# Widening the weight-sum matmuls of the shared key slot from 32 to 64 columns in a masked-attention and two-layer kernel

## The chip, the cores and the metric

The kernel runs on one core of one Trainium2 chip. The metric is the device time of one execution in microseconds (us); lower is better. Engines are named as in the profile: PE (TensorE matmul), PEld (its weight loads), DVE (VectorE), ACT (ScalarE), POOL (GpSimd), SP (the engine that issues the transfers).

## The reference

Attention over 4 batches x 8 heads, 576 positions, head size 64. Scores under a threshold below the row's maximum are dropped before the softmax. Its result (2304 tokens x 512) goes through two layers, each up to 2048 and down to 512: softplus in the first, squared ReLU in the second.

```python
scores = scale * np.matmul(q, k.transpose(0, 1, 3, 2))
thresh = np.max(scores, axis=-1, keepdims=True) - tau
scores = np.where(scores >= thresh, scores, -1000000000.0)
scores = scores - np.max(scores, axis=-1, keepdims=True)
attn = np.exp(scores)
attn = attn / (np.sum(attn, axis=-1, keepdims=True) + 1e-09)
return np.matmul(attn, v)
...
g = np.maximum(h, 0.0) + np.log1p(np.exp(-np.abs(h)))   # first layer, h = x @ w_in
...
r = np.maximum(h, 0.0); g = r * r                       # second layer
return g @ w_out
```

## The kernel before, in words

**Units.** The attention is cut into 32 units. A unit is one batch, one half of the query positions (288 of 576) and one pair of heads. Keys lie on the 128 partitions, queries along the free axis. Of a head's 576 keys, 512 fill four slots of 128 partitions. The last 64 keys of both heads share one slot: head 0 has partitions 0 to 63, head 1 has 64 to 127. So a unit's weights after the exponential, tile `st` (called `e` in the code that reads it), have nine slots of 128 x 288: 0 to 3 for head 0, 4 the shared one, 5 to 8 for head 1.

**Output of a unit (`a_out`).** Two PSUM banks take it. Bank `a_ps[0]` (X) sums weights times values: head 0 on partitions 0 to 63, head 1 on 64 to 127. Bank `a_ps[1]` (D) sums the weights alone with a tile of ones, `one_t`: head 0 on partitions 64 to 127, head 1 on 0 to 63. In D each head has two strips of 32 partitions: slots c = 0 and 2 are summed in one, 1 and 3 in the other. The shared slot adds to the first strip only. Later the two strips are read by DVE and ACT (lines 440 to 444), added and inverted.

The matmuls of a unit come in this order on PE, or with the first two groups exchanged, as the planner has it:

- L420: 8 matmuls, 128 rows x 64 columns of the array, into X.
- L427: 8 matmuls, 128 rows x 32 columns, into D, four strips in turn.
- L432 and L433, the shared slot, for head 0 and then head 1: one matmul into X of 64 rows x 64 columns, one into D of 64 rows x 32 columns. All four are one entry of the plan, so that nothing comes between them.

These matmuls are in full float32, and the trace shows each as two MATMUL and two LDWEIGHTS records. The text calls the two the passes of a matmul. The shared slots of all units make 4 matmuls x 2 passes x 32 units = 256 MATMUL records. The rows of the trace write the shape of the array as rows\*columns (64\*32).

**Around it.** An attention unit's weights are made by scores on PE (L364, L369), copied out by ACT (L372), reduced to a maximum by DVE, the maximum goes through DRAM to all partitions, DVE subtracts and thresholds (L402, L405), ACT takes the exponential (L406). The output of unit u is worked out two units after its scores. ACT then copies X and D out (L435, L437); DVE works out the reciprocals (L440 to L446) and scales (L447). Between units' matmuls stand those of the first layer: up (L463 to L465), softplus on ACT and DVE, a split into a high and a low part (ACT L481; DVE or POOL L482), and down (L494 to L496). The second layer has the rest of the time, from about 716 us on.

**What sets the order.** A planner (`Plan`) takes each operation with a cost written into the code and lists them once per engine; the chip runs each engine's list in that order, and semaphores do the rest. The shared slot has the cost 590 ns there.

Of the kernel before, what the change touches and what calls it, by code (L numbers as in the profile page):

```python
# [9 lines left out]
F32 = mybir.dt.float32  # L10
# [6 lines left out]
B, H, S, D = 4, 8, 576, 64  # L17
# [200 lines left out]
def kernel(ctx: ExitStack, tc: tile.TileContext, qT, kT, vp, tau, w1i, w1o, w2i, w2o, out):  # L218
    nc = tc.nc
    w1i, w1o, w2i, w2o = (w.bitcast(U32) for w in (w1i, w1o, w2i, w2o))  # L220
    PE, ACT, DVE, POOL, SP = nc.tensor, nc.scalar, nc.vector, nc.gpsimd, nc.sync
# [37 lines left out]
    ap = att.enter_context(tc.tile_pool(name="att", bufs=1))  # L259
# [14 lines left out]
    NX = 5  # L274
    xf_t = many(NX, [128, HALF], "xf")
    w_t = ap.tile([128, 18], F32, name="w_t")
    one_t = ap.tile([128, 32], F32, name="one_t")
    POOL.memset(one_t, 1.0)
    m_d = [dram.tile([18, 32], F32, name=f"m_d{i}") for i in range(4)]


# [126 lines left out]
    def a_out(u, key):  # L408
        cold = COLD if u < NCOLD else 1
        e, E = st_t[u % 3], [("st", u % 3, o) for o in range(2)]  # L410
        vt, V = v_t[u % 2], ("v", u % 2)
        xf, XF = xf_t[u % NX], ("xf", u % NX)
        rb, RB = rb_t[0], "rb"
        half = [slice(0, 64), slice(64, 128)]
        X, D = a_ps[0][:, :HALF], a_ps[1][:, :HALF]
        AX0, AD = ("a", 0), ("a", 1)
        for c in range(4):
            def mms(c=c):
                for o in range(2):
                    PE.matmul(X[64 * o:64 * o + 64], vt[:, 256 * o + 64 * c:256 * o + 64 * c + 64], e[:, 5 * o + c], start=(c == 0), stop=False)  # L420
            P.add("PE", (490 + 100 * (c == 0)) * cold, mms, E + [V], [AX0], key)
        for c in range(0, 4, 2):
            def mms(c=c):
                for o in range(2):
                    for i in range(2):
                        a = 64 - 64 * o + 32 * i
                        PE.matmul(D[a:a + 32], one_t, e[:, 5 * o + c + i], start=(c == 0), stop=(c == 2 and i == 1))  # L427
            P.add("PE", (490 + 100 * (c == 0)) * cold, mms, E, [AD], key)

        def mms():  # L430
            for o, h in enumerate(half):
                PE.matmul(X[h], vt[h, 512:], e[h, 4], start=False, stop=True)  # L432
                PE.matmul(D[64 - 64 * o:96 - 64 * o], one_t[h], e[h, 4], start=False, stop=True)  # L433
        P.add("PE", 590 * cold, mms, [E[0], V], [AX0, AD], key)
        P.add("ACT", 310, lambda: ACT.copy(xf, X), [AX0], [XF], key - 0.5)  # L435
        for o in range(2):
            P.add("ACT", 310, lambda o=o: ACT.copy(rb[half[o]], D[half[1 - o]]), [AD], [RB], key - 0.5)  # L437

        d, DN = d_t[u % 2], ("d", u % 2)
        P.add("DVE", 380, lambda: DVE.tensor_reduce(d[:, 0], rb.rearrange("p (b i) -> p b i", i=32), axis=AX.X, op=ALU.max, apply_transpose=True), [RB], [DN], key + 1)  # L440
        for a in range(4):
            b = a ^ 1
            P.add("ACT", 220, lambda a=a, b=b: ACT.copy(d[32 * a:32 * a + 32, 1], d[32 * b:32 * b + 32, 0]), [DN], [("d2", u % 2)], key + 0.5)
        P.add("DVE", 140, lambda: DVE.scalar_tensor_tensor(out=d[:, 0], in0=d[:, 0], scalar=1e-9, in1=d[:, 1], op0=ALU.add, op1=ALU.add), [("d2", u % 2)], [DN], key + 1)
        P.add("DVE", 140, lambda: DVE.reciprocal(d[:, 0], d[:, 0]), [], [DN], key + 1)
        P.add("DVE", 380, lambda: DVE.transpose(rb, d[:, 0].unsqueeze(2).to_broadcast([128, 9, 32])), [DN], [RB], key + 1)  # L446
        P.add("DVE", 375, lambda: DVE.tensor_tensor(xf, xf, rb, op=ALU.mult), [RB], [XF], key + 1, lock=True)  # L447
# [67 lines left out]
    with tc.manual_schedule():  # L515
# [5 lines left out]
        for s in range(last1 + 1):  # L521
# [18 lines left out]
            while wpos < len(wlist) and wpos < 2 * (s + 1):  # L540
                src, f, o = wlist[wpos]
# [152 lines left out]
```

## Time and profile before

| | us |
|---|---|
| median of 3 runs | 1174.6 |
| lowest, highest | 1174.29, 1176.4 |
| the profiled execution's own time | 1177.02 |
| its span, first to last instruction | 1175.2 |

Mean granted TensorE clock of the profiled execution: 0.988 of full speed. The span is what the trace covers; 1.8 us of the execution's own time lie around it. Below, "the stretch 230 to 716" is from 230 us to 716 us after the span's start.

### The profile page before, as it was taken

The page shows a single profiled execution, that of the slowest core. Times are in us where ns is not written, and L with a number is a line of the kernel's source. Part 1 is how long each engine was busy: PE and PEld are TensorE (multiplying, and loading weights), DVE is VectorE, ACT ScalarE, POOL GpSimd, SP SyncE. Part 2 cuts the span into 40 slices and gives each one's busy share as a digit, 9 for nine tenths or more (in the row PEclk, how much of TensorE's full clock was granted, in tenths as well). Part 3 has the DMA queues.
Part 4 walks back from the last instruction along what each step waited for, and adds up shares of the span by engine and source line. Part 5 has one row for each costly group of instructions (what it writes and reads, how often), then busy time and mean ns, then how long its engine had stood idle before and what let it go on. Part 6 is the DMA issues. An engine that isn't in the chain of part 4 may idle for free.

```text
span 1175.2 us, 18185 instructions
## 1 busy us (share of the span) xinstructions
PE 1145.8 (98%) x6992; PEld 887.8 (76%) x6992; DVE 698.6 (59%) x992; ACT 690.8 (59%) x1640; POOL 245.6 (21%) x209
## 2 busy tenths in 40 slices
PE   7779999999999999999999999999999999999998
PEld 3335777877877877877777879988888888888887
DVE  5999986766776666657656745889322322222232
ACT  6787887777777776777677657865322222222222
POOL 1024223332332232333223211444000000000000
PEclk9888999999999999999999999999999999999999
DMA  5365422112112112112111004765010010000010
GB/s 190 109 200 181 140 89 84 46 44 81 46 39 83 41 45 83 39 48 74 47 48 42 31 11 146 212 205 159 7 66 1 1 54 1 1 37 1 1 37 19
DMA packets 39291, 81.85 MB, mean 70 GB/s; under 512 B 6180, under 2 KB 14884, under 8 KB 39204
## 3 DMA queue, kind: packets, MB, share of 16 engines
q1 hardware_dynamic: 39204, 80.69, 21.6%
q8 instruction: 55, 0.90, 0.3%
q14 instruction: 32, 0.26, 0.1%
HBM read 71.17 MB, written 9.50 MB: 69 GB/s over the span
## 4 chain that ended last, share of the span: by engine, by line
PE 90%; DVE 4%; ACT 3%; DMA 1%; issue 0%; SPq 0%; ACTq 0%; DVEq 0%
PE h_ps L463 12%; PE h_ps L464 11%; PE h_ps L465 11%; PE y_ps L494 6%; PE y_ps L604 6%; PE y_ps L603 6%; PE y_ps L605 6%; PE y_ps L496 5%; PE y_ps L495 5%; PE a_ps L364 5%; PE a_ps L420 5%; PE a_ps L432 3%; PE a_ps L433 3%; PE a_ps L427 3%; DVE st L402 1%; PE a_ps L369 1%
## 5 line engine op out<-in xcount | busy, mean ns | idle before, releaser
L482 POOL TENSOR_TENSOR g_l<-gt,g_h 128x288 fp32r<-128x288 f32 x96 | 102.8, 1074 | 316.4 <-ACT g_h L481 278.8
L463 PE MATMUL h_ps<-x_h,wih 128*128 128x288 f32 x512 | 160.1, 313 | 0.7 <-DVE gt L476 0.7
L494 PE MATMUL y_ps<-g_h,woh 128*128 128x288 f32 x512 | 158.2, 309 | 0.0
L464 PE MATMUL h_ps<-x_l,wih 128*128 128x288 f32 x512 | 150.5, 294 | 1.2 <-DVE x_l L454 1.2
L465 PE MATMUL h_ps<-x_h,wil 128*128 128x288 f32 x512 | 151.6, 296 | 0.0
L496 PE MATMUL y_ps<-g_l,woh 128*128 128x288 f32 x512 | 151.1, 295 | 0.0
L495 PE MATMUL y_ps<-g_h,wol 128*128 128x288 f32 x512 | 150.9, 295 | 0.0
L402 DVE TENSOR_TENSOR st<-st,mb 64x288 f32<-64x288 f32 (+1 forms) x128 | 129.0, 1022 | 3.3 <-DMA mb<-m_d 2.2
L583 ACT ACTIVATE r<-h_ps 128x512 f32<-128x512 f32 (+1 forms) x80 | 44.5, 556 | 146.2 <-PE h_ps L465 145.8
L584 DVE SCALAR_TENSOR_TENSOR r<-h_ps,r 128x512 f32<-128x512 f32 (+1 forms) x80 | 51.0, 638 | 131.8 <-ACT r L583 131.6
L464 PE MATMUL h_ps<-y_l,wih 128*128 128x512 f32 (+1 forms) x320 | 120.1, 375 | 0.1
L590 ACT CAST g_h<-r 128x512 fp32r<-128x512 f32 (+1 forms) x80 | 46.2, 578 | 125.4 <-PE y_ps L604 125.4
L463 PE MATMUL h_ps<-y_h,wih 128*128 128x512 f32 (+1 forms) x320 | 119.2, 372 | 0.0
L465 PE MATMUL h_ps<-y_h,wil 128*128 128x512 f32 (+1 forms) x320 | 118.7, 371 | 0.0
L591 DVE TENSOR_TENSOR g_l<-r,g_h 128x512 fp32r<-128x512 f32 (+1 forms) x80 | 51.7, 646 | 110.9 <-ACT g_h L590 110.8
L604 PE MATMUL y_ps<-wol,g_h 128*128 128x512 f32 x288 | 114.1, 396 | 0.0
L603 PE MATMUL y_ps<-woh,g_h 128*128 128x512 f32 x288 | 114.1, 396 | 0.0
L605 PE MATMUL y_ps<-woh,g_l 128*128 128x512 f32 x288 | 114.0, 396 | 0.0
L463 PEld LDWEIGHTS h_ps<-x_h,wih 128*128 128x128 f32 x512 | 96.4, 188 | 21.9 <-issue 18.7
L494 PEld LDWEIGHTS y_ps<-g_h,woh 128*128 128x128 f32 x512 | 96.4, 188 | 16.4 <-issue 15.3
L405 DVE SCALAR_TENSOR_TENSOR st<-st,thr 128x1152 f32<-128x1152 f32 (+1 forms) x64 | 104.1, 1628 | 0.1
L476 DVE SCALAR_TENSOR_TENSOR gt<-h_ps,a_t 128x288 f32<-128x288 f32 x128 | 57.4, 450 | 77.3 <-ACT a_t L475 73.9
(102 smaller groups left out, 2410.5 us busy)
## 6 DMA issues: line engine op xcount, KB each, us to landing
k_r<-in_kT SPq DMA_DIRECT2D x32, 320.0 KB
v_t<-in_vp SPq DMA_DIRECT2D x32, 288.0 KB
wraw<-in_w1i SPq DMA_DIRECT2D x16, 512.0 KB
wraw<-in_w1o SPq DMA_DIRECT2D x16, 512.0 KB
wraw<-in_w2i SPq DMA_DIRECT2D x16, 512.0 KB
wraw<-in_w2o SPq DMA_DIRECT2D x16, 512.0 KB
mb<-m_d SPq DMA_DIRECT2D x28, 288.0 KB
q_r<-in_qT SPq DMA_DIRECT2D x32, 144.0 KB
```

Of the source, the lines that this page charges most:

```text
L402: DVE.tensor_tensor(st[p0:p1, a:a + n], st[p0:p1, a:a + n], mb[p0:p1, o:o + 1].to_broadcast([p1 - p0, n, HALF]), op=ALU.subtract),
L405: P.add("DVE", 315 * (s1 - s0), lambda x=x: DVE.scalar_tensor_tensor(out=x, in0=x, scalar=thr, in1=x, op0=ALU.is_lt, op1=ALU.subtract), [] ...
L463: PE.matmul(bank, wih[p][:, c, f], xh[c], start=(c == 0), stop=False)
L464: PE.matmul(bank, wih[p][:, c, f], xl[c], start=False, stop=False)
L465: PE.matmul(bank, wil[p][:, c, f], xh[c], start=False, stop=(c == 3))
L482: P.add(eng, ns, lambda j=j: e.tensor_tensor(g_hl[1][j], gt_t[j], f32(g_hl[0][j]), op=ALU.subtract), [("gt", j), ("g_h", j)], [("g_l", j)] ...
L494: PE.matmul(o, woh[p][:, j, es], g_h[j], start=first, stop=False)
L495: PE.matmul(o, wol[p][:, j, es], g_h[j], start=False, stop=False)
L496: PE.matmul(o, woh[p][:, j, es], g_l[j], start=False, stop=last)
L603: PE.matmul(o, g_h[j][:, ts], woh[p][:, j], start=first, stop=False)
L604: PE.matmul(o, g_h[j][:, ts], wol[p][:, j], start=False, stop=False)
L605: PE.matmul(o, g_l[j][:, ts], woh[p][:, j], start=False, stop=last)
```

## The change

The ones tile gets 64 columns: 32 ones and 32 zeros. It is filled by two POOL instructions instead of one. The matmuls of L427 take its first 32 columns, as before. The two of the shared slot that sum the weights (L433) take all 64 columns and write 64 partitions of D: the first strip of the head gets the sum, and zeros are added to its second strip. The mark that ends an accumulation moves from L427 to L433. No cost and no entry of the plan is changed: on PE, DVE, ACT and SP every instruction keeps its place; the 64 weight-sum matmuls have 64 partitions out in place of 32, and POOL has one instruction more near its start.

```diff
-    one_t = ap.tile([128, 32], F32, name="one_t")
-    POOL.memset(one_t, 1.0)
+    one_t = ap.tile([128, 64], F32, name="one_t")
+    POOL.memset(one_t, 0.0)
+    POOL.memset(one_t[:, :32], 1.0)
...
-                        PE.matmul(D[a:a + 32], one_t, e[:, 5 * o + c + i], start=(c == 0), stop=(c == 2 and i == 1))
+                        PE.matmul(D[a:a + 32], one_t[:, :32], e[:, 5 * o + c + i], start=(c == 0), stop=False)
...
                 PE.matmul(X[h], vt[h, 512:], e[h, 4], start=False, stop=True)
-                PE.matmul(D[64 - 64 * o:96 - 64 * o], one_t[h], e[h, 4], start=False, stop=True)
+                PE.matmul(D[64 - 64 * o:128 - 64 * o], one_t[h], e[h, 4], start=False, stop=True)
```

So the four matmuls of the shared slot have these rows and columns of the array: before, X of head 0 (rows 0-63, columns 0-63), D of head 0 (0-63, 64-95), X of head 1 (64-127, 64-127), D of head 1 (64-127, 0-31); after, the second and the fourth have columns 64-127 and 0-63.

## Rows read from the trace of the kernel before

**Rows 1.** The page: busy us of each engine, share of the span, instructions.

```profile
PE 1145.8 (98%) x6992; PEld 887.8 (76%) x6992; DVE 698.6 (59%) x992; ACT 690.8 (59%) x1640; POOL 245.6 (21%) x209
```

**Rows 2.** Busy time in three stretches: stretch, length, engines' busy us, granted clock, DMA.

```profile
0.00:125.00 125.00, 101.06 (x487) 54.10 (x487) 110.32 (x145) 99.15 (x242) 27.11 (x26) 0.89 0.51 165
125.00:230.00 105.00, 104.25 (x754) 78.51 (x753) 86.36 (x129) 81.81 (x206) 31.87 (x25) 1.00 0.30 91
230.00:330.00 100.00, 100.00 (x739) 78.53 (x738) 65.83 (x94) 74.00 (x193) 31.66 (x26) 1.00 0.17 55
```

**Rows 3.** One shared slot, PE in order of time, pass by pass: start, us.

```profile
580.59 0.45 PE L432 MATMUL a_ps<-st,v_t 64*64 64x288 f32 x1
580.88 0.40 PE L432 MATMUL a_ps<-st,v_t 64*64 64x288 f32 x1
581.22 0.43 PE L433 MATMUL a_ps<-st,one_t 64*32 64x288 f32 x1
581.48 0.40 PE L433 MATMUL a_ps<-st,one_t 64*32 64x288 f32 x1
581.82 0.45 PE L432 MATMUL a_ps<-st,v_t 64*64 64x288 f32 x1
...
583.04 0.40 PE L494 MATMUL y_ps<-g_h,woh 128*128 128x288 f32 x1
```

**Rows 4.** Passes of L427, L420 and L364, in order of time: start, us.

```profile
575.61 0.45 PE L427 MATMUL a_ps<-st,one_t 128*32 128x288 f32 x4
575.88 0.43 PE L427 MATMUL a_ps<-st,one_t 128*32 128x288 f32 x4
...
576.36 0.43 PE L427 MATMUL a_ps<-st,one_t 128*32 128x288 f32 x4
576.72 0.40 PE L369 MATMUL a_ps<-q_h,k_h 128*128 128x288 f32 x1
...
579.03 0.41 PE L420 MATMUL a_ps<-st,v_t 128*64 128x288 f32 x2
579.28 0.41 PE L420 MATMUL a_ps<-st,v_t 128*64 128x288 f32 x2
...
586.82 0.40 PE L364 MATMUL a_ps<-q_h,k_h 64*128 64x288 f32 x2
```

**Rows 5.** All weight loads and passes of L432 and L433: min/median/max ns.

```profile
L432 PEld LDWEIGHTS a_ps<-st,v_t x128: 129/131/133, 36.5 to 704.7; 64*64 64x64 f32 x128
...
L433 PEld LDWEIGHTS a_ps<-st,one_t x128: 102/104/106, 37.1 to 705.3; 64*32 64x32 f32 x128
```

**Rows 6.** The chain that ended last, near the fourth and fifth shared slots: start, us.

```profile
78.36 4.35 DMA wraw<-in_w1o
...
83.50 0.40 ACT rb L437
...
106.26 0.63 PE a_ps L432 x2
```

**Rows 7.** L433 alone in two stretches: stretch, length, PE busy, PEld busy.

```profile
0.00:125.00 125.00, 6.69 (x20) 1.34 (x20) 0.89 0.51 165
125.00:230.00 105.00, 6.69 (x20) 1.34 (x20) 1.00 0.30 91
```

**Rows 8.** Exponentials on ACT and their first readers on PE, ninth and 23rd unit.

```profile
193.76 1.27 ACT L406 ACTIVATE st<-st,qsc 128x1152 f32<-128x1152 f32 x1
...
195.08 0.45 PE L427 MATMUL a_ps<-st,one_t 128*32 128x288 f32 x4
...
502.10 1.50 ACT L406 ACTIVATE st<-st,qsc 128x1440 f32<-128x1440 f32 x1
...
507.86 0.45 PE L427 MATMUL a_ps<-st,one_t 128*32 128x288 f32 x4
```

**Rows 9.** Waits in the stretch 230 to 716: us in total, times, longest.

```profile
ACT rb L437 <- PE a_ps L433: 67.9, 21, 6.5
```

**Rows 10.** Low parts made by POOL: all as a group; one, and its reader.

```profile
L482 POOL TENSOR_TENSOR g_l<-gt,g_h 128x288 fp32r<-128x288 f32 x96 | 102.8, 1074 | 316.4 <-ACT g_h L481 278.8
...
536.36 2.84 POOL L482 TENSOR_TENSOR g_l<-gt,g_h 128x288 fp32r<-128x288 f32 x1 [6.68 <-DVE st L402]
...
539.37 0.29 PE L496 MATMUL y_ps<-g_l,woh 128*128 128x288 f32 x1
```

**Rows 11.** The tile of ones: the fill on POOL.

```profile
L278 POOL MEMSET one_t<- x1: 114/114/114, 1.4 to 1.4; 128x32 f32 x1
```

## The prediction, made before the changed kernel was run

> **What bounds the kernel now.** I read the busy times first. PE is busy 1145.8 us of the span, DVE and ACT some 60% each [rows 1]. An average can hide stages, so the next view is the table of stretches [rows 2]. It shows three parts of the attention phase. From 0 to 125 us PE is busy 101.06 of 125 us and DVE 110.32: here DVE, ACT and transfers lead. From 125 to 230 PE is nearly full, but DVE (86.36 of 105) and ACT (81.81) are not far behind. In the third row, and in those like it up to 716 us, PE is full, DVE has about a third free and ACT a quarter. There a microsecond taken from PE is a microsecond off the end, as long as nobody else is late. The granted clock is 1.00 from 125 us on, the upper level of 2.4 GHz.
>
> Then the one place that the change touches, pass by pass [rows 3]. The shared slot begins at 580.59 and the next work starts at 583.04: 2.45 us for eight passes. The reader should see that no two passes start together. Within one matmul the second pass starts 0.29 us after the first (580.59 to 580.88), and the next matmul, which has another shape, starts 0.34 us after that (580.88 to 581.22). Compare the weight sums of the full slots [rows 4]: four passes on four different column strips start together at 575.61, four more at 575.88, and the fourth such round starts at 576.36, two rounds after the second. So sixteen passes take four rounds, 0.24 us apart, and the next shape begins 0.36 us after the last round (576.72). L420, with two tiles of 64 columns, goes in rounds of two every 0.25 us. L364, with two row tiles, starts two together as well. So passes on different tiles of one shape run side by side here, and where the shape changes they don't.
>
> **The change part by part.** *The shared slot.* Afterwards its four matmuls have one shape, 64\*64, and the four lie on four different quarters of the array. If they behave like the four strips of L427, the first passes start together, the second passes 0.29 us later (the gap in [rows 3]), and the next shape 0.34 us after that. That makes 0.63 us; L427's rounds give 0.27 + 0.36 = 0.63 too. I add 0.02 for a spread of the starts, my choice: 0.65. The slot falls from 2.45 to 0.65 us, 1.80 us a unit. No row has four tiles of 64\*64, so both ends: at best 0.61 (the gaps of the narrower L433, 0.26 from 581.22 to 581.48 and 0.34 from 581.48 to 581.82, give 0.60); at worst all eight passes one after another, priced under the rivals. I take the value near the best because L427, L420 and L364 [rows 4] all run their tiles side by side, and L427 and L364 between them show both ways of cutting, columns and rows.
>
> *Dearer loads.* L433's weight loads take 104 ns at 32 columns, L432's 131 ns at 64 [rows 5]. That is 27 ns for each of 128 loads, 3.5 us if nothing hid them. In L427 and L420 rounds follow each other at 0.24 to 0.25 us with loads in between, so I cost them at nothing; without that cover they are the 3.5 us.
>
> *The second fill.* It stands on POOL beside one that takes 114 ns at 1.4 us [rows 11], some 35 us before the first pass of L433 [rows 5]. Nothing; if it were on the path, 0.1 to 0.2 us.
>
> *Added zeros, later end mark.* No instruction more on PE, and the readers of D waited for L433 already [rows 9]. Nothing.
>
> *What becomes of 1.80 us a unit.* A unit has four passes of L433. Twenty of the 128 fall in the stretch 0 to 125, twenty in 125 to 230 [rows 7], so five units each, and 22 units behind that. I make three groups.
>
> Units 1 to 4: the chain does not run through their slots. At the fourth it lies on a transfer of weights from 78.36 to 82.71 [rows 6], while the slot runs. I count 0; if all counted it were 4 x 1.80 = 7.2.
>
> Units 5 to 10: the fifth slot is the first on the chain, at 106.26 [rows 6], and from there the slots are on PE's full stretch, but the exponential comes hardly earlier than PE wants it. In the ninth unit it ends at 193.76 + 1.27 = 195.03, and its first reader starts at 195.08 [rows 8]. A PE that arrives 1.80 us earlier waits. ACT and DVE do start earlier behind a shorter slot, so not all is lost. Between 0 and 10.8 us I take the middle: 5.4.
>
> Units 11 to 32, 22 of them: 39.6 us. Here the margin is large. The smallest that I found among the 22 is at unit 23: the exponential ends at 502.10 + 1.50 = 503.60 and is read at 507.86, 4.26 us later [rows 8]. Between a unit's scores and its output lie the slots of two other units, so a faster PE can use up at most 3.6 us of it, even if the whole chain through ACT and DVE took no profit. And it does profit: in this stretch ACT's next copy waited 67.9 us, in 21 waits, for the last pass of the slot [rows 9], so ACT moves up along with PE. What can bite is the hand-over inside the first layer. Mostly it has microseconds to spare, but POOL's low part that ends at 536.36 + 2.84 = 539.20 is read at 539.37, 0.17 us later [rows 10]. I take off a tenth, 4.0 us, as an estimate for such places: 35.6.
>
> *Sum:* 0 + 5.4 + 35.6 = 41.0 us. The profiled execution's own time of 1177.02 becomes 1136.0. It stood 2.4 us above the median of the runs, 1174.6, so I forecast **1133.6 us**. Everything counted, 32 x 1.80 = 57.6, would give 1117.0; the second stretch at 0 and a quarter lost in the third, 29.7, gives 1144.9.
>
> **The rivals.**
>
> *Two at a time.* Both matmuls into X write one bank, from different halves of the rows, and so do both into D. L364's two row tiles, which do run together, write two different banks; L427's four strips share a bank but have all the rows. So no row shows two row tiles in one bank at once. If the bank holds the second row tile back, the order X, D of head 0, then X, D of head 1 gives two pairs of rounds: 0.29 + 0.24 + 0.25 + 0.34 = 1.12 us. The saving is 1.33 a unit; weighed as above, 41.0 x 1.33 / 1.80 = 30.3, or 1144.3 us. For it: the gap in the rows just named. Against it: the two write different partitions, as L427's strips do, and those don't hold each other back. The Trainium skill's page TensorEngine Tiling, section Restrictions and Gotchas, bears on this: it says that different row tiles cannot access the same PSUM bank simultaneously, and leaves the order to software. By that rule the slot would be the 1.12 us just given; the trace of before neither shows nor breaks it.
>
> *One after another.* The tiles gain nothing from a common shape, only the waits at the three changes of shape inside the slot shrink: 0.29 + 6 x 0.245 + 0.34 = 2.10 us. That saves 0.35 a unit, 41.0 x 0.35 / 1.80 = 8.0 us, 1166.6. This is the case in which the change doesn't do what it says. Against it stand all the rounds of [rows 4].
>
> *Eaten by DVE and ACT.* The slot shortens, but PE then waits for exponentials or low parts. Shorter by 41 us or so, the 125 to 716 stretch would ask for more of DVE and ACT in each microsecond, and POOL's work beside DVE stretches (2.84 us for one that takes 1.07 in the mean of 96 [rows 10]). If half of the third group's and nothing of the second's came through: 19.8 us, 1154.8. Against it: the free third of DVE and quarter of ACT [rows 2].
>
> *Slower.* If two passes on different row halves of one bank must not only wait but drain, as at a change of shape, each pass costs 0.34: 8 x 0.34 = 2.72 us, 0.27 more than now, over the 28 units whose slot is on PE's full stretch 7.6 us: 1182.2. It decides from 2.45 / 8 = 0.306 us a pass on. Against it: L432's two passes into one bank already follow each other at 0.29.
>
> **How the numbers follow.** Chances: as forecast 0.65 (its own range 1117 to 1142), two at a time 0.17 (1144 or so), eaten 0.07, one after another 0.06, slower 0.05. The range 1117 to 1149 holds the first two, apart from what of either falls below 1117 or above 1149, 0.8 in all. Within 0.2% (2.3 us, about what a measurement of this kernel can tell from no change) only the tail of two rivals falls: 0.03. Faster by more: 0.92; slower by more: 0.05.
>
> **What would show it.** Pass by pass, the shared slot should have four starts within some 0.05 us, four more 0.29 us later, and the next shape 0.34 us after those, in all 32 units. Two starts in each of four rounds mean the bank rival; eight starts 0.24 us apart the serial one. L433's weight loads should go from 104 to about 131 ns. In what is now the stretch 230 to 716, the periods of the units should shrink by about 1.6 to 1.8 us with PE still full. If PE is no longer full there, and its waits name L406, L482 or L476, the loss is in the hand-over and I have mis-sized the tenth. The part from the end of the attention on should take as long as before. The prediction is wrong above all if the tiles don't run four at a time, and next if the early units, where DVE and ACT are near their limit, give more or less than half.

## The result, and the profile after

The changed kernel took **1126.3 us** (median of 4 runs, 1125.5 to 1127.9), the kernel before 1175.5 in the same comparison. The ratio is 0.958, with a 95% interval of 0.956 to 0.960: 49.2 us faster. The forecast was 1133.6 with the range 1117 to 1149; the direction and the range held, and the forecast gain of 41.0 us was 8 too small. The span of the profiled execution fell from 1175.2 to 1124.4, by 50.8 us; the profiled execution of the kernel before, 1177.02, lies 1.5 above the median, so the leads read from the two traces below are about that much too large.

The line numbers of the changed kernel are one higher from L278 on: L432 is now L433, and L433 is L434.

First the page of the changed kernel, busy us by engine:

```profile
PE 1088.9 (97%) x6992; PEld 872.7 (78%) x6992; DVE 698.4 (62%) x992; ACT 690.0 (61%) x1640; POOL 247.4 (22%) x210
```

Against [rows 1] the busy time of PE fell by 56.9 us and that of its weight loads by 15.1; DVE, ACT and POOL stayed within 2 us of where they were. The number of PE instructions is the same: nothing was left out, the same passes lie side by side.

Now the shared slot itself, pass by pass, of the same unit as in [rows 3] (start, us; PE in order of time):

```profile
542.45 0.45 PE L433 MATMUL a_ps<-st,v_t 64*64 64x288 f32 x1
542.46 0.45 PE L434 MATMUL a_ps<-st,one_t 64*64 64x288 f32 x1
542.47 0.45 PE L433 MATMUL a_ps<-st,v_t 64*64 64x288 f32 x1
542.47 0.45 PE L434 MATMUL a_ps<-st,one_t 64*64 64x288 f32 x1
542.75 0.40 PE L433 MATMUL a_ps<-st,v_t 64*64 64x288 f32 x1
542.75 0.40 PE L434 MATMUL a_ps<-st,one_t 64*64 64x288 f32 x1
542.76 0.40 PE L433 MATMUL a_ps<-st,v_t 64*64 64x288 f32 x1
542.77 0.40 PE L434 MATMUL a_ps<-st,one_t 64*64 64x288 f32 x1
543.10 0.40 PE L495 MATMUL y_ps<-g_h,woh 128*128 128x288 f32 x1
```

The reader should see four starts within 0.02 us, four more 0.29 us later, and the next shape at 543.10. From 542.45 to 543.10 are 0.65 us, where [rows 3] had 2.45. In 30 of the 32 units the slot measures 0.64 or 0.65 us to the start of the next work. The eight passes of the other two look the same, but behind them PE has to wait for DVE: behind the first slot (1.60 us) and behind the 13th (1.06 us). The row behind the 13th slot, which began at 271.09:

```profile
272.14 0.40 PE L464 MATMUL h_ps<-x_h,wih 128*128 128x288 f32 x1 [0.34 <-DVE gt L477]
```

The stretches answer to [rows 2] (stretch, length, engines' busy us, granted clock, DMA):

```profile
0.00:125.00 125.00, 95.19 (x504) 51.99 (x505) 111.47 (x152) 101.18 (x249) 26.42 (x27) 0.86 0.53 166
125.00:220.00 95.00, 94.26 (x747) 76.65 (x746) 85.40 (x123) 80.89 (x203) 31.66 (x25) 1.00 0.33 101
...
420.00:520.00 100.00, 100.00 (x795) 81.62 (x795) 70.96 (x101) 78.34 (x205) 34.83 (x30) 1.00 0.22 64
```

The stretch 420 to 520 of the kernel before:

```profile
420.00:520.00 100.00, 100.00 (x732) 75.23 (x731) 64.46 (x91) 70.57 (x184) 32.70 (x27) 1.00 0.19 57
```

PE is still as good as full from 125 us on. DVE and ACT do the same work in less time, so their shares rose (ACT from 71 to 78 of 100, DVE from 64 to 71), and from 220 us on neither stops PE except behind the 13th slot. In the first 125 us the granted clock was 0.86, against 0.89 before.

Where the time came from is seen from the starts of four slots, the first, the sixth, the 11th and the last. The kernel before:

```profile
36.45 0.45 PE L432 MATMUL a_ps<-st,v_t 64*64 64x288 f32 x1
...
136.00 0.45 PE L432 MATMUL a_ps<-st,v_t 64*64 64x288 f32 x1
...
246.32 0.45 PE L432 MATMUL a_ps<-st,v_t 64*64 64x288 f32 x1
...
703.39 0.45 PE L432 MATMUL a_ps<-st,v_t 64*64 64x288 f32 x1
```

The changed kernel:

```profile
34.92 0.45 PE L433 MATMUL a_ps<-st,v_t 64*64 64x288 f32 x1
...
133.54 0.45 PE L433 MATMUL a_ps<-st,v_t 64*64 64x288 f32 x1
...
234.83 0.45 PE L433 MATMUL a_ps<-st,v_t 64*64 64x288 f32 x1
...
654.40 0.45 PE L433 MATMUL a_ps<-st,v_t 64*64 64x288 f32 x1
```

The lead is 1.53 us when the first slot starts, 2.46 at the sixth, 11.49 at the 11th, 48.99 at the last. From the sixth slot to the 11th it grows by 9.03 in five units, 1.81 each; from the 11th to the last by 37.50 in 21 units, 1.79 each. So behind the fifth unit every slot handed on the whole of its 1.80 us but one, the 13th, where the lead grew by 1.39. What the first five slots gave can't be read here: a lead of 1.53 was there before any of the wide matmuls ran.

### The profile page after: what moved, and what is told of

Read it like the earlier page. It is cut to its first block, busy times and chain, and to the rows that moved or that the text cites. A ratio compares the mean times of both kernels' runs of the same rounds, so it can differ in the third digit from the quotient of the medians.

```text
span 1124.4 us, 18186 instructions
## 1 busy us (share of the span) xinstructions
PE 1088.9 (97%) x6992; PEld 872.7 (78%) x6992; DVE 698.4 (62%) x992; ACT 690.0 (61%) x1640; POOL 247.4 (22%) x210
## 4 chain that ended last, share of the span: by engine, by line
PE 89%; DVE 5%; ACT 4%; DMA 1%; issue 1%; SPq 0%; DVEq 0%; ACTq 0%
PE h_ps L464 13%; PE h_ps L465 12%; PE h_ps L466 12%; PE y_ps L495 7%; PE y_ps L604 6%; PE y_ps L605 6%; PE y_ps L606 6%; PE y_ps L497 6%; PE y_ps L496 6%; PE a_ps L421 6%; PE a_ps L365 5%; PE a_ps L428 3%; PE a_ps L433 1%; DVE st L403 1%; PE a_ps L370 1%; DVE m L380 1%
## 5 line engine op out<-in xcount | busy, mean ns | idle before, releaser
L465 PE MATMUL h_ps<-x_l,wih 128*128 128x288 f32 x512 | 150.4, 294 | 1.5 <-DVE x_l L455 1.5
L592 DVE TENSOR_TENSOR g_l<-r,g_h 128x512 fp32r<-128x512 f32 (+1 forms) x80 | 51.6, 646 | 111.0 <-ACT g_h L591 110.9
L465 PE MATMUL h_ps<-y_l,wih 128*128 128x512 f32 (+1 forms) x320 | 120.1, 375 | 0.0
L373 ACT ACTIVATE st<-a_ps 128x288 f32<-128x288 f32 x234 | 84.8, 404 | 23.8 <-PE a_ps L365 14.6
```

Source lines behind the costliest of these rows:

```text
L465: PE.matmul(bank, wih[p][:, c, f], xl[c], start=False, stop=False)
```

## The experiments

Six kernels were run, each compared with the kernel before on the same chip.

**Three groups of units.** Three kernels have the wide form in some of the units only, to see what each group of my sum was worth. The edit in the first of them (the others have `5 <= u < 10` and `u >= 10`; all three set the end mark of L427 where the old form needs it):

```diff
-                PE.matmul(D[64 - 64 * o:128 - 64 * o], one_t[h], e[h, 4], start=False, stop=True)
+                w = 64 if u < 5 else 32
+                PE.matmul(D[64 - 64 * o:64 - 64 * o + w], one_t[h, :w], e[h, 4], start=False, stop=True)
```

Expected of units 1 to 5:

> Only units 1 to 5 have the 64-column form, the others the old one. In the trace of the changed kernel the lead over the kernel before was 1.72 us at the start of the fifth slot and 2.46 us at the sixth. Theory (each slot on PE's path gives its full 1.80 us, and the slots of the first four give little because DVE, ACT and transfers lead there): 1.5 to 3 us faster than before. Rival (my prediction's weights, 0 for four units and half for the fifth): 0.9 us faster. Rival (the ten missing microseconds came from the early units): over 6 us faster.

Expected of units 6 to 10:

> Only units 6 to 10 have the 64-column form. Theory (the exponential, late as it is, moves up with PE, so that nothing of 5 x 1.80 is lost): 9.0 us faster than before. Rival (the prediction's half): 4.5 us faster. Rival (the gain there needed the head start of units 1 to 5): under 7 us.

Expected of units 11 to 32:

> Only units 11 to 32 have the 64-column form. Theory (no hand-over costs anything): 22 x 1.80 = 39.6 us faster, less at most 0.5. Rival (the prediction's tenth is lost in hand-overs of the first layer): 35.6 us faster. If the three groups add up to the 50.8 us by which the changed kernel's span is shorter, the gains do not depend on one another.

| wide form in | ratio to before, 95% | gain at 1175.7 us | forecast for the group | all of 1.80 us a slot |
|---|---|---|---|---|
| units 1 to 5 | 0.9996, 0.9986 to 1.0007 | 0.5 (-0.8 to 1.6) | 0.9 | 9.0 |
| units 6 to 10 | 0.9926, 0.9910 to 0.9942 | 8.7 (6.8 to 10.6) | 4.5 | 9.0 |
| units 11 to 32 | 0.9669, 0.9652 to 0.9686 | 38.9 (36.9 to 40.9) | 35.6 | 39.6 |

The groups add up to 48.1 us, the whole change gave 49.2: within the error they don't depend on one another, and the late gain needs no head start. The rival in which the missing microseconds came from the early units has fallen, and so has my half for units 6 to 10. Units 11 to 32 gave all of their slots' time within the error; a loss of a tenth lies outside the interval, if not by much. Of units 1 to 5 my theory expected 1.5 us at least, and the measured gain can't be told from nothing; here the prediction's 0.9 did better, though 1.5 lies just inside the interval.

That units 6 to 10 need no head start either is clearer from their trace than from the time, whose interval reaches down to 6.8 us. Their sixth and 11th slots start here:

```profile
135.24 0.45 PE L433 MATMUL a_ps<-st,v_t 64*64 64x288 f32 x1
...
236.48 0.45 PE L433 MATMUL a_ps<-st,v_t 64*64 64x288 f32 x1
```

The lead over the kernel before grows from 0.76 to 9.84 us, 1.82 a unit.

In the trace of the kernel with units 1 to 5, the sixth, 11th and last slots start as follows:

```profile
134.72 0.45 PE L433 MATMUL a_ps<-st,v_t 64*64 64x288 f32 x1
...
245.02 0.45 PE L433 MATMUL a_ps<-st,v_t 64*64 64x288 f32 x1
...
702.13 0.45 PE L433 MATMUL a_ps<-st,v_t 64*64 64x288 f32 x1
```

Its lead over the kernel before is 1.28, 1.30 and 1.26 us. A lead that PE has at the sixth slot arrives at the end unchanged, through 570 us of hand-overs: a sign that nothing behind the sixth slot runs on a time of its own. A lead this small at that point is no proof of a gain, though. In the kernels with units 6 to 10 and 11 to 32, whose early slots are as before, PE also led by 0.76 and 0.25 us at the sixth slot, and by up to 2.1 us at some before it.

**Order instead of width.** The old 32 columns, but both X matmuls first and both D matmuls behind them:

```diff
...
             for o, h in enumerate(half):
                 PE.matmul(X[h], vt[h, 512:], e[h, 4], start=False, stop=True)
-                PE.matmul(D[64 - 64 * o:128 - 64 * o], one_t[h], e[h, 4], start=False, stop=True)
+            for o, h in enumerate(half):
+                PE.matmul(D[64 - 64 * o:96 - 64 * o], one_t[h, :32], e[h, 4], start=False, stop=True)
```

> The old 32-column form, but the slot's matmuls in another order: both into X (64 rows x 64 columns, two row tiles in one bank), then both into D (64 x 32). Theory (passes on different tiles of one shape run together, a change of shape ends that): two starts together, 0.29 us later two more, a change of shape, and the same again for D: 0.63 + 0.60 = 1.23 us a slot, 1.22 saved in some 27 to 28 units: 33 to 35 us faster than before. Rival (the zeros' width is what lets the tiles run together): as before. Rival (two row tiles in one bank wait for each other where the shape of the weights, not the order, had to change): 0.29 + 3 x 0.245 + 0.34 = 1.37 for X and 1.3 for D, no gain or a loss.

Measured: 1142.6 us against 1175.7, ratio 0.971 (0.970 to 0.973), 33.2 us faster. One of its slots, in order of time:

```profile
445.71 0.46 PE L433 MATMUL a_ps<-st,v_t 64*64 64x288 f32 x2
...
446.00 0.41 PE L433 MATMUL a_ps<-st,v_t 64*64 64x288 f32 x2
446.34 0.43 PE L435 MATMUL a_ps<-st,one_t 64*32 64x288 f32 x2
...
446.61 0.41 PE L435 MATMUL a_ps<-st,one_t 64*32 64x288 f32 x2
446.95 0.40 PE L465 MATMUL h_ps<-x_h,wih 128*128 128x288 f32 x1
```

Two starts together, two more 0.29 us later, a change of shape 0.34 us behind, and the same again: 1.24 us. So two thirds of the gain are to be had without any wider tile, by not alternating shapes. And the two X matmuls, two row tiles in one bank, start at one time: the ground of my bank rival is gone.

**One shape, but two tiles.** Here all four matmuls have 64 rows x 64 columns as in the changed kernel, but a head's two lie on the same quarter of the array:

```diff
-                        a = 64 - 64 * o + 32 * i
+                        a = 64 * o + 32 * i
...
-                PE.matmul(D[64 - 64 * o:128 - 64 * o], one_t[h], e[h, 4], start=False, stop=True)
+                PE.matmul(D[64 * o:64 * o + 64], one_t[h], e[h, 4], start=False, stop=True)
...
-            P.add("ACT", 310, lambda o=o: ACT.copy(rb[half[o]], D[half[1 - o]]), [AD], [RB], key - 0.5)
+            P.add("ACT", 310, lambda o=o: ACT.copy(rb[half[o]], D[half[o]]), [AD], [RB], key - 0.5)
```

> The changed kernel with the weight sums of a head in the same partitions of their bank as its output in the other, so that in the shared slot a head's two matmuls lie on one quarter of the array: all four still have one shape, 64 x 64, but only two quarters are used. Theory (one shape is not enough, the tiles must be different ones; each tile takes its passes in turn): rounds of two passes, 0.29 + 0.24 + 0.25 + 0.34 = 1.12 us a slot, 0.47 us more than 0.65, in 28 units 13 us slower than the changed kernel, some 37 us faster than before. Rival (one shape is what counts): 0.65 us a slot, as the changed kernel. Rival (passes start in the order of the program, so that the second head waits for the first): 1.8 to 1.9 us a slot, some 34 us slower than the changed kernel.

Measured: 1139.8 us against 1175.7, ratio 0.970 (0.969 to 0.971), 35.9 us faster. One of its slots:

```profile
443.18 0.47 PE L433 MATMUL a_ps<-st,v_t 64*64 64x288 f32 x2
...
443.47 0.41 PE L433 MATMUL a_ps<-st,v_t 64*64 64x288 f32 x2
443.72 0.42 PE L434 MATMUL a_ps<-st,one_t 64*64 64x288 f32 x2
...
443.96 0.41 PE L434 MATMUL a_ps<-st,one_t 64*64 64x288 f32 x2
444.30 0.40 PE L464 MATMUL h_ps<-x_h,wih 128*128 128x288 f32 x1
```

Four rounds of two, 1.12 us in all, as the theory had it. One shape alone is not what counts; the tiles must be different ones. The two heads run side by side though head 0's two matmuls stand ahead of head 1's in the kernel, so the rival of strict order has fallen too. Beside the kernel with the other order this one also shows the price of a change of shape by itself: from the second round to the third are 0.25 us here (443.47 to 443.72), 0.34 there.

**Is PE still the bound?** The slot's matmuls are left out, so that the last 64 keys of each head add nothing to the output; the plan keeps its entry, so the order of all else stays. The end marks move to the matmuls ahead (not shown).

```diff
...
-        def mms():
-            for o, h in enumerate(half):
-                PE.matmul(X[h], vt[h, 512:], e[h, 4], start=False, stop=True)
-                PE.matmul(D[64 - 64 * o:128 - 64 * o], one_t[h], e[h, 4], start=False, stop=True)
-        P.add("PE", 590 * cold, mms, [E[0], V], [AX0, AD], key)
+        P.add("PE", 590 * cold, lambda: None, [E[0], V], [AX0, AD], key)
```

> The shared slot's matmuls are left out, so the last 64 keys of each head add nothing to the output; all else keeps its order. Theory (PE still leads from the fifth unit on and the other engines move up with it): another 0.65 us a unit over some 27.5 units, 18 us faster than the changed kernel (span about 1106). Rival (DVE and ACT, busy 71 to 79 us of 100 now, start to hold PE up): under 12 us.

Measured: 1110.1 us against 1175.7, ratio 0.944 (0.943 to 0.945). That is 16.2 us under the changed kernel, 1126.3. The units 6 to 32, 27 x 0.65 = 17.6, would explain all of it and 1.4 more, which is within the runs' scatter. Against the kernel before the gains are 65.6 (64.4 to 67.4) and 49.2 (47.0 to 51.6), so even the ends that lie nearest leave 12.8 between them, and the rival's 12 is excluded. A stretch of this kernel, columns as above:

```profile
410.00:510.00 100.00, 100.00 (x784) 83.35 (x783) 73.12 (x105) 81.00 (x213) 33.93 (x31) 1.00 0.22 67
```

PE is full even here; from 125 to 655 us it waited 1.7 us for DVE, in three waits, and 0.5 for ACT. What is left of the slot after the change is still paid at the end, nearly one for one.

## Why the prediction was right, and where its size was off

**The slot: right.** 0.65 us was forecast and 0.65 measured, four starts and then four, with the spread of 0.02 that I had added. The reasoning from L427, L420 and L364 [rows 4], which each show one way of cutting the array, carried over to both ways at once.

**Dearer loads, second fill, end mark: nothing, right.** All weight loads of L434 in the changed kernel (min/median/max ns):

```profile
L434 PEld LDWEIGHTS a_ps<-st,one_t x128: 129/130/133, 34.9 to 654.5; 64*64 64x64 f32 x128
```

L434's loads went from 104 to 130 ns, as forecast, and the rounds did not move apart.

**Units 6 to 10 at half, units 11 to 32 less a tenth: the two terms that were mis-sized.** With the fifth unit counted to its neighbours as in the sum, the forecast gave 5.4 + 35.6; measured were 8.7 for units 6 to 10 and 38.9 behind them. Both discounts rested on one reading: a small margin between an engine's result and PE's use of it was taken for a wait about to open. The same two places in the changed kernel show why that was wrong. First the exponential and its reader in the ninth unit, then in the 23rd (ACT and PE in order of time):

```profile
185.87 1.26 ACT L407 ACTIVATE st<-st,qsc 128x1152 f32<-128x1152 f32 x1
...
187.20 0.45 PE L428 MATMUL a_ps<-st,one_t 128*32 128x288 f32 x4
...
469.39 1.50 ACT L407 ACTIVATE st<-st,qsc 128x1440 f32<-128x1440 f32 x1
...
475.10 0.45 PE L428 MATMUL a_ps<-st,one_t 128*32 128x288 f32 x4
```

In the ninth unit the margin was 0.05 us [rows 8] and is 187.20 - 187.13 = 0.07 now, though PE comes 7.88 us earlier. In the 23rd it was 4.26 and is 4.21, though PE comes 32.76 us earlier. Then POOL's low part, its reader, and the answer to [rows 10]:

```profile
500.04 2.83 POOL L483 TENSOR_TENSOR g_l<-gt,g_h 128x288 fp32r<-128x288 f32 x1 [4.93 <-DVE st L403]
...
503.04 0.29 PE L497 MATMUL y_ps<-g_l,woh 128*128 128x288 f32 x1
```

539.37 - 539.20 = 0.17 before, 503.04 - 502.87 = 0.17 now. At these places the producers moved up as far as their reader, to within 0.05 us. Why the exponential does is to be read from the chain of the kernel before, just ahead of 193.76 where it starts, and from two rows beside the chain, a wait of ACT and the last step of DVE on the exponential's input:

```profile
191.70 0.15 PE h_ps L465
191.84 0.02 issue
191.87 0.41 ACT a_t L473
192.28 0.30 ACT st L372
192.58 0.33 ACT a_t L474
192.91 0.30 ACT a_t L473
...
189.67 0.41 ACT L372 ACTIVATE st<-a_ps 128x288 f32<-128x288 f32 x1 [0.82 <-PE a_ps L364]
...
191.86 1.42 DVE L405 SCALAR_TENSOR_TENSOR st<-st,thr 128x1152 f32<-128x1152 f32 x1
```

ACT's queue stands behind matmuls of PE's own (L364, for which it sat idle 0.82 us, and L465), and the exponential has its place a few entries further on in that queue; its input was ready at 191.86 + 1.42 = 193.28, 0.48 us before it started. Released earlier by PE, ACT is earlier by the same amount. For POOL's low part the runs show only that it moved, not through which engine. I had this argument for the third group, by ACT's waits [rows 9], and still discounted; ACT's waits for the last pass of the slot fell as well, in the stretch from 220 to 667 us, from the 67.9 us of [rows 9] to this (and 4.3 us more, in one wait, ahead of its copy of X):

```profile
ACT rb L438 <- PE a_ps L434: 34.3, 18, 4.8
```

One hand-over of the first layer did open, as the prediction feared, and it measured 0.41 us where 4.0 had been taken off. It is the one behind the 13th slot. Before and after (DVE's work, then its reader on PE, which in the changed kernel is the row at 272.14 shown above):

```profile
286.78 0.42 DVE L476 SCALAR_TENSOR_TENSOR gt<-h_ps,a_t 128x288 f32<-128x288 f32 x1
...
288.65 0.40 PE L463 MATMUL h_ps<-x_h,wih 128*128 128x288 f32 x1
...
271.67 0.42 DVE L477 SCALAR_TENSOR_TENSOR gt<-h_ps,a_t 128x288 f32<-128x288 f32 x1
```

DVE starts this work 0.58 us after the slot's start in both kernels (286.20 and 271.09), so it moved up by all that the earlier slots had saved, but it can gain nothing from the slot beside which it runs. Its margin was 288.65 - 287.20 = 1.45 us, the slot saves 1.80, and PE waits the difference and the 0.05 us from DVE's end (272.09) to its own start. The margin of such work has to outlast the saving of one slot, not the sum of all.

**Units 1 to 4 at nothing: right.** The run of units 1 to 5 gave 0.5 us, with nothing inside the interval. The first 125 us of its trace:

```profile
0.00:125.00 125.00, 94.01 (x498) 52.23 (x499) 110.25 (x148) 99.98 (x246) 25.97 (x27) 0.88 0.52 165
```

PE is busy 7 us less than in [rows 2] and no earlier at the end: what the slots gave became idle time of PE, while DVE is busy 110 us as before. Which of DVE, ACT, the transfers and the slightly lower granted clock (0.88 against 0.89) holds the end of this stretch was not separated.

**The rivals.** *Two at a time* fell twice: by the slot's rows, and by the kernel that puts both X matmuls together. The rule behind it, in the Trainium skill's page TensorEngine Tiling (Array Packing), section Restrictions and Gotchas, says that different row tiles cannot access the same PSUM bank simultaneously. Here X of head 0 and X of head 1 do so, with starts 542.45 and 542.47, on different partitions of the bank, and the output is right; the measurement decides, for row tiles whose columns, and so whose partitions of the bank, differ. Row tiles that write the same partitions of a bank were not tried. *One after another* fell by the same rows. *Eaten by DVE and ACT* fell by the stretches and by the kernel without the slot. *Slower* needed a drain of 0.34 us between passes on different row halves; they start 0.02 us apart.

**The sum.** 0.5 + 8.7 + 38.9 = 48.1 by the groups where the forecast had 41.0; the whole change gave 49.2.

## What to carry to other kernels

Where small matmuls alternate between two shapes of the array, give them one shape and different tiles, if need be by padding the smaller with zero columns: eight passes of 288 columns went from 2.45 to 0.65 us, and sorting by shape alone brought them to 1.24. To judge whether a gain on the bounding engine survives, don't count small margins behind other engines as losses; look at what released those engines, and where it is the bounding engine itself, ahead of the place that got shorter, the margin travels along. Work that was released already and runs beside the shortened place keeps its time, so there compare its margin with what that one place saves. And where the bounding engine has idle time, as in the first 125 us here, the gain can be nothing: 0.5 us measured (at most 1.6) of the 9.0 that five slots saved.

## What the runs showed of the hardware that was not expected

Passes don't start in the order in which the kernel lists the matmuls. In the kernel with two tiles, head 1's first pass starts with head 0's (443.18), ahead of head 0's second matmul (443.72), which stands before it in the code, and in the compiled list of PE's instructions too; the rows read as if each tile took its own passes in turn.

Passes of 64 rows x 64 columns are not slowed when three others run beside them: four first passes and four second ones keep the 0.29 us between them and the 0.34 us to the next shape that one pass at a time showed in [rows 3]. The profile's own durations, a median of 428 ns for the passes into X in both kernels, can't show it, since it models the ends of matmuls.
